# Moving a float64 weight conversion between two stages of a fused mLSTM, mixture-of-experts and gated MLP kernel, and letting one block's second products trail by two steps

## The chip, the core and the metric

The kernel runs on one core of a Trainium2 chip. The metric is the device time of one execution in microseconds (us), from the median of several runs. The engines are called by their short names: PE (TensorE, the matrix products), ACT (ScalarE), DVE (VectorE), POOL (GpSimd) and SP (SyncE, which here only issues transfers).

## What is computed

Three layers run one after the other on 3072 tokens of width 320. The change touches the second and the third; the first, a recurrent attention (mLSTM), is not touched.

```python
# second layer: eight experts, each token goes to one of them (x: 3072 x 320, F = 1024)
for e in range(E):
    mask = expert_idx == e
    h = np.maximum(x[mask] @ w1[e], 0.0)
    out[mask] = gate_w[mask, None] * (h @ w2[e])
...
# third layer: a gated MLP (w_in: 320 x 2048, w_out: 2048 x 320)
h = x @ w_in
g = h * (1.0 / (1.0 + np.exp(-1.702 * h)))
return (g @ w_out).astype(np.float32)
```

The third layer's weights `w_in` and `w_out` come as float64, because they are drawn in float32 and then multiplied by a float64 factor; the kernel has to turn their bits into float32 itself.

## The kernel before

All products are made in float32 accuracy from fp32r pieces: each operand is split into a rounded high part and a rest, and three products (high by high, high by low, low by high) are summed in PSUM. So every weight and every activation costs a copy on ACT (the high part) and a subtraction on DVE or POOL (the rest).

**Experts.** There are 64 steps `s`, eight experts `e` of eight steps `m`. The first four experts work on up to 512 tokens, the last four on up to 384 (`CAPS`). A step makes the first products of one slice of 128 hidden columns (`h_mm`, line 138, eight matmuls into the PSUM tile `hp`, of which there are two), then the relu and its split (`relu_split`: `hh` on ACT, line 1093, and `hl` on DVE, line 1094), then the second products of the slice of the step before (`tail`, `o_mm`, lines 1117 to 1119, into the PSUM tiles `acc`). After that the same step splits a weight slice for a later step (`split_w`: lines 105 and 118 on ACT, 110 on POOL, 111 and 121 on DVE), transposes the next expert's tokens in three of the eight steps (`prep_x`), and calls `convert`.

**Conversion.** `cvt_all` is a generator over the 16 column blocks of `w_in` and `w_out`. A block needs 10 pieces, five for its `w_in` part (128x384) and five for its `w_out` part (128x320); `convert(n)` runs the next n pieces. The first piece is `fr` and `es` on ACT (lines 1158 and 1161) with `ex` on DVE between them (line 1159; `es` reads `ex`); the other four are one DVE operation each (`mt` 1163, `fr` 1165, `es` 1167, `fr` 1169). When the fifth piece is done, the split of the finished weights is put on the list `late`, and the next `convert` runs it (the same lines 105 to 121, now into `win` and `wout`). The float64 words are loaded to the tile `c` by SP (line 1177), two such tiles in turn. In all 160 pieces: the experts run `convert(2 + m % 2)` for 512 tokens and `convert(1 + m % 2)` for 384, from step 2 on.

**Gated MLP.** Five blocks of 512 tokens and two of 256, each with 16 steps. A step of a block is `h_mm`, then `swish_split`: ACT makes the sigmoid `sg` (line 1104), DVE multiplies it with `hp` (line 1105, which frees `hp`), ACT rounds the product to `hh` (line 1106) and DVE subtracts for `hl` (line 1107). Then come the second products of an earlier step, taken from the list `left`. A step of a 512-token block costs PE eight first and twelve second matmuls. The first block, number `E`, runs what is left of the conversion beside its products, three pieces a step, and also prepares the second block: `scale_y` (line 1246, on POOL), and from the sixth step on `planes` (1268), `words` (1277) and `parts` (1285 and 1286).

Nothing here is ordered by a scheduler: under `tc.manual_schedule` each engine works through its instructions in the order in which the code is written, and waits on semaphores for what it reads or overwrites.

Of the kernel before, what the change touches and what calls it, by code (L numbers as in the profile page):

```python
# [20 lines left out]
CAP = 512  # L21
# [5 lines left out]
def kernel(ctx, tc, qT_in, kT_in, kvo_in, i_gate, f_gate, expert_emb, tau, w12, wio, out, dbg=None):  # L27
# [5 lines left out]
    E = expert_emb.shape[0]  # L33
# [18 lines left out]
    CAPS = [CAP] * (E // 2) + [CAP - P] * (E // 2)  # L52
# [33 lines left out]
    def load_w(g):  # L86

        p, m = divmod(2 * g, M1)
        r1, r2 = w_dma(ids[p], m // 2, rawp.tile([P, W2], F32, tag="r", name="r"))
        wraw[2 * g], wraw[2 * g + 1] = (r1[:, :, 0:P], r2[:, 0]), (r1[:, :, P:2 * P], r2[:, 1])  # L90
# [915 lines left out]
    with ExitStack() as mctx:  # L1006
# [16 lines left out]
        def load_x0(j):  # L1023

            if j:
                xr_t["first"] = xp.tile([P, NB, 3 * P], F32, tag="xr", name="xr", bufs=1)
                t = xr_t["first"][:, 0:NB // 2]
            else:
                t = mp2.tile([P, NB, DM], F32, tag="o", name="xr", bufs=1).rearrange("p i d -> p (i d)")
                t = t[:, 0:NB // 2 * 3 * P].rearrange("p (i d) -> p i d", d=3 * P)  # L1030
            xr_t["first", j] = t
            src = rows[ds(ids[0] * RS + j * EARLY, EARLY), :].rearrange("(i p) d -> p i d", p=P)
            nc.sync.dma_start(out=t[:, :, 0:DM], in_=src)
# [8 lines left out]
        ncol = lambda blk: GN if blk == "g" else COLS[blk]  # L1042
# [15 lines left out]
        def prep_x0(j, c):  # L1058

            if j and c == 0:  # L1060
                xh_t[0] = mp2.tile([P, 3, CAP], F32R, tag="xh", name="xh")
                xl_t[0] = mp2.tile([P, 3, CAP], F32R, tag="xl", name="xl")
            xh, xl, xr = xh_t[0], xl_t[0], xr_t["first", j]
            js = slice(2 * j * P, (2 * j + 2) * P)
            if c == 0:
                nc.scalar.copy(xr[:, :, DM:3 * P], xr[:, :, 2 * P:DM])
            pool, tag = (ps_h, "hp") if j and c == 2 else (ps_x, "xt")
            t = pool.tile([P, CAP], F32, tag=tag, name="xt")[:, 0:2 * P]
            for i in range(2):
                nc.tensor.transpose(t[:, i * P:(i + 1) * P], xr[:, i, c * P:(c + 1) * P], ident)  # L1070
            nc.scalar.copy(xh[:, c, js], t)
            nc.vector.tensor_tensor(out=xl[:, c, js], in0=t, in1=xh[:, c, js].bitcast(F32), op=ALU.subtract)

        def touch():

            xr, n = xr_t["first", 1], 3 * P - DM
            t = ps_x.tile([P, CAP], F32, tag="xt", name="xt")
            nc.tensor.matmul(t[:, 0:n], ident, ident[:, 0:n], start=True, stop=True)
# [300 lines left out]
        with tc.manual_schedule():  # L1379
            load_x0(1)  # L1380
            flag = nc.values_load(vals_i[0:1, 2 * E:2 * E + 1], min_val=0, max_val=1)
            with tc.If(flag > 0):
                general()
            touch()
            nc.vector.memset(exb, -896.0 * 2 ** 23)
            load_x0(0)
            for p in range(1, E):
                ids[p] = nc.values_load(vals_i[0:1, p:p + 1], engines=sp, min_val=0, max_val=E - 1)
                if p == 1:
                    load_w(WA // 2 + 1)  # L1390
                    for c in range(3):
                        prep_x0(1, c)
                    load_x(1)
                    load_w(WA // 2 + 2)
                    load_c(0)
                    load_c(1)
            offs = {p: nc.values_load(vals_i[0:1, E + p:E + p + 1], engines=sp, min_val=0, max_val=NT) for p in range(1, E)}

            steps = [(e, m, e * M1 + m) for e in range(E) for m in range(M1)]
            prev = None  # L1400
            conv = cvt_all()

            def convert(n):

                now, late[:] = late[:], []
                for f in now:
                    f()
                for _ in range(n):
                    next(conv, None)

            def tail(p):
                e, m, s = p
                o_mm(e, ("a", s), wslot.pop(s)[1], m == 0, m == M1 - 1)
                if m == M1 - 1:
                    put(e)

            for e, m, s in steps:
                h_mm(e, ("a", s), wslot[s][0], EARLY if s in he else 0)
                relu_split(("a", s))
                if s in he:  # L1420
                    hs_t["a", s] = halves(*he.pop(s)) + hs_t["a", s]
                if prev:
                    tail(prev)
                prev = (e, m, s)
                if 1 <= s < 4:
                    prep_x0(0, s - 1)
                if s == 1:
                    gts = gates_1()
                if s == 2:
                    gates_2(*gts)  # L1430
                if s == 3:
                    order_rows()
                if s == 4:
                    meta_tile()

                for w in [] if s == 0 else [s + WA - 1] if s < WA else [s + WA - 1, s + WA] if s == WA else [s + WA]:
                    if w < NS1:
                        split_w(w)
                        if w % 2 and w // 2 + 3 < NS1 // 2:
                            load_w(w // 2 + 3)  # L1440
                if e + 1 < E and 2 <= m - (e == 0) < 5:
                    prep_x(e + 1, m - 2 - (e == 0))
                if m == 5 + (e == 0) and e + 2 < E:
                    load_x(e + 2)
                if s % 2 == 0 and 0 <= s // 2 - 3 < NTILE:
                    meta_put(s // 2 - 3)
                if s == 7 + 2 * NTILE:
                    meta_get()
                if s == 9 + 2 * NTILE:
                    meta_split()  # L1450
                if e == E - 1:

                    if m == 1:
                        load_y(E)
                    if m == 3:
                        scale_y(E, nc.vector)
                    if 4 <= m < 7:
                        prep_x(E, m - 4)
                    if m == 7:
                        load_y(E + 1)  # L1460

                if s > 1:
                    convert((1 if CAPS[e] < CAP else 2) + m % 2)

            def tail2(p):
                blk, m = p
                o_mm(blk, ("b", blk, m), wout[:, m], m == 0, m == M2 - 1)
                if m == M2 - 1:
                    put_out(blk)

            left = [prev]
            for blk in range(E, len(COLS)):
                for m in range(M2):
                    h_mm(blk, ("b", blk, m), win[:, m])
                    swish_split(("b", blk, m))
                    left.append((blk, m))
                    while len(left) > (1 if ncol(blk) == CAP else 2):
                        p = left.pop(0)
                        (tail2 if len(p) == 2 else tail)(p)
                    if blk == E:  # L1480
                        convert(3)
                    nxt = blk + 1
                    if nxt < len(COLS):
                        t = m - (2 if blk == E else 0)
                        small = ncol(blk) < CAP
                        if t == 2:
                            scale_y(nxt, nc.vector if small else nc.gpsimd)
                        for j in range(ncol(nxt) // GH):
                            t0 = t - 3 * j
                            if 3 <= t0 < 5:  # L1490
                                planes(nxt, j, t0 - 3)
                            w0 = t0 - (8 if small else 6)
                            if 0 <= w0 < 2:
                                words(nxt, j, w0)
                            if 2 <= w0 < 5:
                                parts(nxt, j, w0 - 2)
                        if t == 8 and nxt + 1 < len(COLS):
                            load_y(nxt + 1)
            for p in left:
                tail2(p)  # L1500
            if dbg is not None:
                nc.sync.dma_start(out=dbg["slot"], in_=slot_i)
                nc.sync.dma_start(out=dbg["lg"], in_=logit_all.rearrange("p t e -> p (t e)"))
                nc.sync.dma_start(out=dbg["ss"], in_=ss_all)
# [62 lines left out]
```

## Time and profile before

| what | value |
|---|---|
| median of 3 runs | 808.52 us (808.39 to 808.96) |
| the profiled execution: its time, its span | 810.2 us, 808.5 us |
| PE busy | 751.4 us, 93% of the span |
| DVE, ACT, POOL busy | 564.4, 354.2, 249.8 us |
| granted TensorE clock, mean | 0.963 of full speed |

The span runs from the first to the last instruction that the profile shows; the execution's own time has 1.7 us more around it. The attention takes the first 205 us or so, the experts run from 210 to 437 us, the first gated block from 437 to 506 us, and the six other blocks fill the rest. Busy shares are averages over stages with different limits, so each stage is read by itself.

### The profile page before, as it was taken

Reading aid. Unit: us, or ns where it says so; the run is one execution under the profiler, and the core shown is the slowest. Engines: PE = TensorE matmul, PEld = TensorE weight load, DVE = VectorE, ACT = ScalarE, POOL = GpSimd, SP = SyncE. Lnnn points to the kernel's source line nnn. Section 1 sums busy time; section 2 is a strip of 40 time slices with the busy share of each in tenths; the row PEclk is TensorE's granted clock in tenths of the full one; section 3 lists DMA queues with packets and bytes.
Section 4 is the critical chain, followed back from the end, with each engine's and each line's share of the span. In section 5 each row is a group of like instructions: output and inputs, shape, how many; then the busy total and the mean of one; then the engine's idle time right before and its main releaser. Section 6 shows DMA issues by size and latency. Waiting matters only on the chain.

```text
span 808.5 us, 13134 instructions
## 1 busy us (share of the span) xinstructions
PE 751.4 (93%) x4708; PEld 692.6 (86%) x4708; DVE 564.4 (70%) x1146; ACT 354.2 (44%) x834; POOL 249.8 (31%) x362
## 2 busy tenths in 40 slices
PE   6899898898779999999999899999999999999995
PEld 6889798888768888889988687898989888899995
DVE  7877999997488888888976776554554454445542
ACT  4343334324356556565654444333334333334442
POOL 4653577775123343444520200300300300102011
PEclk9787999899899999999999999999999999999998
DMA  6976876652637637557843122120120110200100
GB/s 195 310 263 206 285 252 224 227 192 86 216 79 252 207 114 237 162 181 205 208 123 104 36 56 59 43 64 6 48 64 1 54 40 9 64 1 21 33 18 16
DMA packets 70303, 100.20 MB, mean 124 GB/s; under 512 B 31120, under 2 KB 56472, under 8 KB 70232
## 3 DMA queue, kind: packets, MB, share of 16 engines
q1 hardware_dynamic: 67160, 91.41, 37.2%
q0 software_dynamic: 3072, 7.89, 2.6%
q8 instruction: 38, 0.62, 0.3%
q14 instruction: 33, 0.27, 0.1%
HBM read 77.53 MB, written 17.82 MB: 118 GB/s over the span
## 4 chain that ended last, share of the span: by engine, by line
issue 37%; DVE 17%; PE 9%; ACT 5%; POOL 4%; DMA 1%; SPq 0%; POOLq 0%; DVEq 0%; ACTq 0%
PE hp L138 4%; DVE w L121 3%; POOL out_dram L1140 3%; DVE w L111 2%; PE acc L1119 2%; DVE hl L1094 2%; DVE es L1167 2%; PE acc L1118 1%; PE acc L1117 1%; DVE fr L1165 1%; ACT hh L1093 1%; DMA c<-in_wio_dram 1%; POOL xr L1246 1%; DVE ex L1159 1%; DVE xl L1056 1%
## 5 line engine op out<-in xcount | busy, mean ns | idle before, releaser
L1105 DVE TENSOR_TENSOR sg<-hp,sg 128x512 f32<-128x512 f32 (+1 forms) x112 | 68.8, 614 | 91.3 <-ACT sg L1104 84.9
L138 PE MATMUL hp<-xh,win 128*128 128x512 f32 (+1 forms) x560 | 131.5, 365 | 0.0
L1117 PE MATMUL acc<-wout,hhl 128*128 128x320 f32 x384 | 119.8, 312 | 4.4 <-ACT hhl L1106 4.3
L1119 PE MATMUL acc<-wout,hhl 128*128 128x320 f32 x384 | 120.4, 314 | 1.1 <-DVE hhl L1107 1.0
L1107 DVE TENSOR_TENSOR hhl<-sg,hhl 128x512 fp32r<-128x512 f32 (+1 forms) x112 | 71.3, 637 | 70.0 <-ACT hhl L1106 69.0
L1118 PE MATMUL acc<-wout,hhl 128*128 128x320 f32 x384 | 119.2, 310 | 0.0
L1104 ACT ACTIVATE sg<-hp 128x512 f32<-128x512 f32 (+1 forms) x112 | 60.0, 536 | 116.2 <-PE hp L138 116.2
L1140 POOL DMA_INDIRECT out_dram<-o,tokd x24 | 23.7, 987 | 273.5 <-ACT o L1127 269.7
L138 PEld LDWEIGHTS hp<-xh,win 128*128 128x128 f32 x560 | 94.3, 189 | 11.4
L1106 ACT CAST hhl<-sg 128x512 fp32r<-128x512 f32 (+1 forms) x112 | 62.6, 559 | 86.7 <-DVE sg L1105 83.2
L138 PE MATMUL hp<-xl,win 128*128 128x512 f32 (+1 forms) x336 | 85.6, 363 | 0.0
L110 POOL TENSOR_TENSOR w<-r,w 128x256 fp32r<-128x256 f32 x58 | 45.7, 788 | 124.5 <-ACT w L105 121.6
L1117 PEld LDWEIGHTS acc<-wout,hhl 128*128 128x128 f32 x384 | 72.7, 189 | 10.4 <-ACT hhl L1106 7.0
L138 PE MATMUL hp<-xh,w 128*128 128x384 f32 (+2 forms) x320 | 76.5, 370 | 0.0
L1119 PEld LDWEIGHTS acc<-wout,hhl 128*128 128x128 f32 x384 | 72.5, 189 | 3.6 <-DVE hhl L1107 3.5
L1118 PEld LDWEIGHTS acc<-wout,hhl 128*128 128x128 f32 x384 | 72.6, 189 | 3.5
L1119 PE MATMUL acc<-w,hl 128*128 128x320 f32 x212 | 68.2, 322 | 6.8 <-DVE hl L1094 6.6
L1117 PE MATMUL acc<-w,hh 128*128 128x320 f32 x212 | 66.5, 314 | 2.4 <-ACT hh L1093 2.4
L138 PEld LDWEIGHTS hp<-xl,win 128*128 128x128 f32 x336 | 58.8, 189 | 10.9 <-DVE xl L1286 0.2
L1118 PE MATMUL acc<-w,hh 128*128 128x320 f32 x212 | 65.7, 310 | 0.0
L360 DVE TENSOR_TENSOR_SCAN pm<-fb,ident_h 128x1024 f32<-128x1024 f32 x23 | 56.3, 2448 | 5.4 <-DMA fb<-dec 5.3
L400 PE MATMUL sp<-qT,kblk 120*128 120x128 f32 x384 | 56.4, 308 | 3.1 <-DVE wm L405 2.7
(315 smaller groups left out, 1522.8 us busy)
## 6 DMA issues: line engine op xcount, KB each, us to landing
r<-in_w_dram SPq DMA_DIRECT2D x32, 704.0 KB
fb<-dec SPq DMA_DIRECT2D x23, 512.0 KB
kvo<-in_kvo_dram SPq DMA_DIRECT2D x24, 480.0 KB
c<-in_wio_dram SPq DMA_DIRECT2D x16, 704.0 KB
rows<-zt SPq DMA_DIRECT2D x8, 640.0 KB
qT<-in_qT_dram SPq DMA_DIRECT2D x24, 180.0 KB
xr<-y SPq DMA_DIRECT2D x5, 640.0 KB
kblk<-in_kT_dram SPq DMA_DIRECT2D x48, 60.0 KB
```

What stands on the lines that cost most here:

```text
L110: eng.tensor_tensor(out=t[:, 3 * P:5 * P].rearrange("p (c f) -> p c f", c=2), in0=r1[:, 0:2], in1=hif[:, 0:2], op=ALU.subtract)
L138: nc.tensor.matmul(hp, a, b, start=(i == 0), stop=(i == len(seq) - 1))
L360: nc.vector.tensor_tensor_scan(out=pm[u].rearrange("p h t -> p (h t)"), data0=fb[u].rearrange("p h t -> p (h t)"), data1=ident_h.rearrange ...
L400: nc.tensor.matmul(sp[:, h - hs.start], kblk[u % NLD][0:KR, h // 3, h % 3, :], qT[u][0:KR, h // 3, :], start=True, stop=True)
L1104: nc.scalar.activation(out=sg, in_=hp, func=AF.Sigmoid, scale=1.702)
L1105: nc.vector.tensor_tensor(out=g, in0=hp, in1=sg, op=ALU.mult)
L1106: nc.scalar.copy(hh, g)
L1107: nc.vector.tensor_tensor(out=hl, in0=g, in1=hh.bitcast(F32), op=ALU.subtract)
L1117: nc.tensor.matmul(a, hh, w[:, 0:DM], start=first, stop=False)
L1118: nc.tensor.matmul(a, hh, w[:, DM:2 * DM], start=False, stop=False)
L1119: nc.tensor.matmul(a, hl, w[:, 0:DM], start=False, stop=last)
L1140: sc = nc.gpsimd.indirect_dma_start(out=out, out_offset=bass.IndirectOffsetOnAxis(ap=tokd[:, ti:ti + 1], axis=0), in_=o[:, i], in_offset=None)
```

## The change

Three numbers and one condition are edited. In the experts the conversion starts at step 4 instead of step 2, and a step runs 2 or 3 pieces by `m % 4 > 0` instead of `m % 2` (1 or 2 for the 384-token experts): three steps in four take the larger number, where it was one in two. In the first gated block a step runs two pieces instead of three. And in this block the list `left` keeps two steps instead of one, so that the second products come two steps behind the first ones; blocks 2 to 5 keep one, the two small ones keep two, as before.

```diff
@@ the loop over the experts' steps
-                if s > 1:
-                    convert((1 if CAPS[e] < CAP else 2) + m % 2)
+                if s > 3:
+                    convert((1 if CAPS[e] < CAP else 2) + (m % 4 > 0))
@@ the loop over the gated blocks
                     left.append((blk, m))
-                    while len(left) > (1 if ncol(blk) == CAP else 2):
+
+                    while len(left) > (1 if E < blk and ncol(blk) == CAP else 2):
                         p = left.pop(0)
                         (tail2 if len(p) == 2 else tail)(p)
                     if blk == E:
-                        convert(3)
+                        convert(2)
```

Counted out, the pieces stand so: before, 15 by the end of step 7, 123 by the end of the experts, and 37 in the first gated block; after, 11, 133 and 27.

What this does to the engines' own order is seen at three places. The first is PE at the passage from the experts to the first gated block (`win` is the gated layer's weight, `w` the experts'). Before:

```order
L1119 MATMUL acc<-w,hl 128x320
L138 MATMUL hp<-xh,win 128x512 x5
L138 MATMUL hp<-xl,win 128x512 x3
L1117 MATMUL acc<-w,hh 128x320
L1118 MATMUL acc<-w,hh 128x320
L1119 MATMUL acc<-w,hl 128x320
```

And now:

```order
L1119 MATMUL acc<-w,hl 128x320
L138 MATMUL hp<-xh,win 128x512 x5
L138 MATMUL hp<-xl,win 128x512 x3
L138 MATMUL hp<-xh,win 128x512 x5
L138 MATMUL hp<-xl,win 128x512 x3
L1117 MATMUL acc<-w,hh 128x320
L1118 MATMUL acc<-w,hh 128x320
L1119 MATMUL acc<-w,hl 128x320
```

The second step's first products now stand ahead of the last expert's second products, and from here to the block's end each step's second products have one more step of first products and one more of second products in front of them.

The second place is DVE in the experts' steps 3 and 4, a piece of the difference (a minus is before, a plus is now):

```order
 L121 TENSOR_TENSOR w<-r,w 128x320
 L1056 TENSOR_TENSOR xl<-xt,xh 128x512
-L1165 SCALAR_TENSOR_TENSOR fr<-mt,fr 128x384
-L1167 SCALAR_TENSOR_TENSOR es<-c,es 128x384
-L1169 TENSOR_TENSOR fr<-fr,es 128x384
 L1094 SCALAR_TENSOR_TENSOR hl<-hp,hh 128x256
 L1219 COPY metat<-tok_i 128x24
```

The three pieces of step 3 are gone from in front of step 4's `hl`; in the same way `ex` and `mt`, the pieces of step 2, are gone from in front of step 3's.

The third place is DVE at the start of the first gated block, from its first multiplication (line 1105) to its third. Before:

```order
L1105 TENSOR_TENSOR sg<-hp,sg 128x512
L1107 TENSOR_TENSOR hhl<-sg,hhl 128x512
L1125 COPY o<-acc 128x320
L1167 SCALAR_TENSOR_TENSOR es<-c,es 128x384
L1169 TENSOR_TENSOR fr<-fr,es 128x384
L1159 TENSOR_SCALAR ex<-c 128x320
L1105 TENSOR_TENSOR sg<-hp,sg 128x512
L1107 TENSOR_TENSOR hhl<-sg,hhl 128x512
L111 TENSOR_TENSOR win<-fr,win 64x128
L1163 TENSOR_SCALAR mt<-c 128x320
L1165 SCALAR_TENSOR_TENSOR fr<-mt,fr 128x320
L1167 SCALAR_TENSOR_TENSOR es<-c,es 128x320
```

And now:

```order
L1105 TENSOR_TENSOR sg<-hp,sg 128x512
L1107 TENSOR_TENSOR hhl<-sg,hhl 128x512
L1167 SCALAR_TENSOR_TENSOR es<-c,es 128x384
L1169 TENSOR_TENSOR fr<-fr,es 128x384
L1105 TENSOR_TENSOR sg<-hp,sg 128x512
L1107 TENSOR_TENSOR hhl<-sg,hhl 128x512
L1125 COPY o<-acc 128x320
L111 TENSOR_TENSOR win<-fr,win 64x128
L1159 TENSOR_SCALAR ex<-c 128x320
L1163 TENSOR_SCALAR mt<-c 128x320
```

One piece a step is gone between two multiplications, and the `ex` of the next column block follows the second step's `win` split instead of ending the first step.

## Rows read from the trace of the kernel before

**Rows 1.** Windows by stage: experts 1-3, experts 4-7, first gated block, second.

```profile
core 0: us, PE busy (x) PEld busy (x) DVE busy (x) ACT busy (x) POOL busy (x), PEclk, DMA share, GB/s
241.80:336.80 95.00, 94.14 (x515) 82.31 (x515) 82.38 (x161) 55.37 (x124) 37.26 (x54) 0.99 0.59 190
336.80:437.10 100.30, 95.55 (x587) 91.54 (x587) 83.28 (x166) 57.99 (x137) 37.33 (x54) 1.00 0.60 169
437.10:505.94 68.84, 63.34 (x320) 52.85 (x318) 49.85 (x93) 32.05 (x64) 6.06 (x5) 0.98 0.22 63
505.94:564.16 58.22, 58.22 (x323) 52.20 (x321) 29.94 (x49) 22.29 (x42) 6.94 (x9) 1.00 0.14 39
```

**Rows 2.** Waits in the first gated block: total us, times, longest.

```profile
PE acc L1117 <- ACT hhl L1106: 4.3, 5, 2.4
```

**Rows 3.** Timeline of the first gated block: start, length, engine, instruction, wait before.

```profile
459.12 2.80 POOL L1246 TENSOR_TENSOR xr<-xr,gated 128x1536 f32<-128x1536 f32 x1
459.32 2.78 DVE L1159 TENSOR_SCALAR ex<-c 128x320 int32<-128x320 int32 x1
464.61 0.42 PE L1117 MATMUL acc<-wout,hhl 128*128 128x320 f32 x1 [2.38 <-ACT hhl L1106]
475.71 0.69 DVE L1105 TENSOR_TENSOR sg<-hp,sg 128x512 f32<-128x512 f32 x1 [0.88 <-ACT sg L1104]
501.37 0.69 DVE L1105 TENSOR_TENSOR sg<-hp,sg 128x512 f32<-128x512 f32 x1 [0.39 <-ACT sg L1104]
505.01 0.69 DVE L1105 TENSOR_TENSOR sg<-hp,sg 128x512 f32<-128x512 f32 x1 [1.24 <-ACT sg L1104]
506.99 0.42 DVE L1286 TENSOR_TENSOR xl<-xt,xh 128x256 fp32r<-128x256 f32 x1
507.11 0.86 PE L138 MATMUL hp<-xl,win 128*128 128x512 f32 x3
```

**Rows 4.** DVE's groups in the first gated block: busy us, mean ns.

```profile
L1165 DVE SCALAR_TENSOR_TENSOR fr<-mt,fr 128x384 f32<-128x384 int32 (+1 forms) x8 | 4.2, 524 | 0.4
L1169 DVE TENSOR_TENSOR fr<-fr,es 128x384 f32<-128x384 f32 (+1 forms) x8 | 4.2, 522 | 0.2
L1167 DVE SCALAR_TENSOR_TENSOR es<-c,es 128x384 int32<-128x384 int32 (+1 forms) x8 | 4.1, 518 | 0.0
L111 DVE TENSOR_TENSOR win<-fr,win 64x128 fp32r<-64x128 f32 x4 | 2.8, 711 | 0.1
L1163 DVE TENSOR_SCALAR mt<-c 128x384 int32<-128x384 int32 (+1 forms) x8 | 2.7, 338 | 0.0
...
L121 DVE TENSOR_TENSOR wout<-fr,wout 128x320 fp32r<-128x320 f32 x4 | 1.9, 484 | 0.0
```

**Rows 5.** Windows around the longest wait of that block; columns as in rows 1.

```profile
464.00:467.00 3.00, 2.23 (x9) 1.96 (x10) 2.32 (x5) 1.50 (x3) 0.00 (x0) 0.76 0.11 17
467.00:470.00 3.00, 3.00 (x12) 2.62 (x11) 1.68 (x3) 1.59 (x4) 0.00 (x0) 0.67 0.87 279
```

**Rows 6.** Timeline of experts' steps 2 to 5: ACT, DVE and PE.

```profile
221.85 0.49 DVE L121 TENSOR_TENSOR w<-r,w 128x320 fp32r<-128x320 f32 x1
222.94 0.56 ACT L1158 ACTIVATE fr<-c 128x384 f32<-128x384 uint32 x1 [2.52 <-DMA c<-in_wio_dram]
224.30 0.42 DVE L1094 SCALAR_TENSOR_TENSOR hl<-hp,hh 128x256 fp32r<-128x256 f32 x1 [0.79 <-ACT hh L1093]
230.66 0.41 PE L1119 MATMUL acc<-w,hl 128*128 128x320 f32 x1 [2.45 <-DVE hl L1094]
```

**Rows 7.** Waits of PE from 204 to 250 us; then a window there.

```profile
PE acc L1119 <- DVE hl L1094: 4.3, 2, 2.5
...
240.00:245.00 5.00, 5.00 (x21) 4.43 (x21) 3.98 (x10) 1.86 (x4) 0.73 (x1) 0.66 0.66 96
```

**Rows 8.** Timeline of expert 4's third step: a first piece and the wait behind it.

```profile
344.85 0.56 ACT L1161 ACTIVATE es<-ex,exb 128x320 int32<-128x320 int32 x1 [2.69 <-DVE ex L1159]
345.84 0.41 PE L1117 MATMUL acc<-w,hh 128*128 128x320 f32 x1 [1.16 <-ACT hh L1093]
```

## The prediction

> **What bounds the kernel now.** I read the windows by stage first. In the second gated block PE is busy for all of its 58.22 us, 16 steps of 3.64 us; the first block does the same work (three second matmuls fewer) in 68.84 us, so about 11 us are lost there [rows 1]. In experts 1 to 7 PE is busy for 94.14 of 95.00 and 95.55 of 100.30 us: 5.6 us idle, with DVE busy for 165.7 of 195.3 us [rows 1]. The second block has no such idle time, and what comes after it is of the same kind, so whatever the first block saves, the end saves too.
>
> Then the waits. In the first gated block PE waits for `hhl`, the rounded activations that ACT writes for the second products, five times, 4.3 us in all [rows 2], the longest 2.38 us [rows 3]; in the timeline the reader sees why. POOL's `scale_y` runs for 2.80 us, and DVE's `ex`, begun 0.2 us later, takes 2.78 us; the sigmoid, the product and the rounding queue up behind it. The clock pays as well: in the 6 us after that wait it is granted at 0.76 and 0.67 [rows 5]. The rest of the 11 us is the same chain in small: sigmoid on ACT, product on DVE, rounding on ACT, rest on DVE, with three conversion pieces between two products.
>
> In expert 0, PE waits 4.3 us for `hl` [rows 7], 2.45 us of it once [rows 6], because ACT and DVE are late there.
>
> **Part 1: the conversion starts at step 4.** By the end of step 7 four pieces fewer have run. A column block of ten pieces costs DVE, by the means in [rows 4] and with `ex` priced like `mt`, 2 x (0.338 + 0.338 + 0.524 + 0.518 + 0.522) + 0.711 + 0.484 = 5.7 us, so 0.57 us a piece and 2.3 us for four. Besides, ACT's first `fr` waits 2.52 us for its data and holds up `hh`: DVE was through at 222.34 (221.85 + 0.49) but began `hl` at 224.30, 1.96 us later [rows 6]. Two steps later the data has long landed. Together 4.3 us; I take **4.0 us off**, since PE's own steps take over as the bound. Ends: 2.0 (only one of the two reaches PE) and 6.0 (the 4.3 us of PE's waits, and the 5 us at clock 0.66 that follow [rows 7], 1.7 us of them lost).
>
> **Part 2: denser conversion from step 8 on.** 122 pieces instead of 108, 14 x 0.57 = 8.0 us more on DVE, which is idle for 29.6 us in this stretch [rows 1]; so most fits, but not at the right moment. What hurts PE is a first piece: ACT's `es` waits for DVE's `ex`, `hh` stands behind `es`, and PE waited 1.16 us for that `hh` [rows 8]. First pieces in these steps go from 22 to 24; two more at 1.16 us are 2.3 us. I take **2.5 us on**, near that row. Ends: nothing (all in DVE's gaps) and 8.0 (all on the path).
>
> **Part 3: two pieces a step and a lag of two in the first gated block.** Both belong together. With the lag, PE reaches the second products of a step one whole step, 3.64 us, later, so a lateness of ACT and DVE up to that size is no wait any more; that alone covers the 2.38 us wait and the small ones. But a lag does not make the chain shorter, it only lends time. `hp` has two buffers, so the first products of step m+2 wait for DVE's product of step m, and at the end the second block's first products read the last `xl` that DVE makes behind the last step. So I take DVE's chain over the whole block. It ends at 507.41 (506.99 + 0.42), just in time for the low products at 507.11 [rows 3], 70.3 us after the block's start. Of these it waited 0.39 and 1.24 us for PE in the last two steps [rows 3]; 68.7 are its own. Ten pieces, one column block, leave it: 5.7 us, and up to two waits of 0.88 us behind an `es` [rows 3], so 5.7 to 7.5; I take 6.5, the middle. The chain then needs 62.2 us and ends at 499.3. The second block's first products began 1.5 us ahead of that end (505.94 against 507.41), so now they begin at 497.8, with one set of twelve second matmuls, half a step or 1.8 us, still to do: as if at 499.6, against 505.94. That is **6.3 us off**; PE alone would have been there 4.7 us sooner. Ends: 4.0 (the chain has waits of its own where two pieces fall badly) and 11 (all that is lost).
>
> The 2.4 us of the `scale_y` stall I leave in this chain. POOL does `scale_y` right behind the `win` split in its queue; that split now comes in the block's second step instead of its fifth, and in DVE's order an `ex` and a `mt` stand behind it there as before. The rule that speaks against the change is about this pair: the Trainium skill's "GPSIMD Engine Reference", section "Key points", says that the two engines share their SBUF interfaces and that DVE instructions in a two-port mode or with two SBUF inputs contend with POOL's. The trace agrees for `ex`: 2.78 us beside POOL [rows 3]. If only `ex` were held and another operation stood there, the sum would be 2.4 us lower, 798.3; by the page `fr`, `es` and the subtraction would be held as well, and the sum stays.
>
> **What costs nothing.** The last expert's second products and its `put` come one step later; their reader is a load nine steps on. The 16 loads of `c` on SP are as many as before; at 2.75 pieces a step a tile lasts 3.6 steps, about 14 us, so SP never brings them late, and if it did, ACT would wait as it does now, 2.5 us [rows 6]. POOL is idle for most of the first gated block, 6.06 of 68.84 us busy [rows 1], so its earlier split and `scale_y` delay nobody there but DVE. The lists and ring buffers gain no instruction.
>
> **Sum.** -4.0 + 2.5 - 6.3 = -7.8 us. The profiled execution took 810.2 us (span 808.5), which gives 802.4 for it; the median of the runs, 808.52, lies 1.7 below and gives **800.7 us**.
>
> **Rivals.**
> - *The lag hides everything.* DVE's chain is shorter than I add up, and the first gated block runs at PE's 3.64 us a step. For: the chain has fewer waits once PE is ahead. Against: even at 7.5 us for the ten pieces it ends 3.7 us late. 808.5 - 4.0 + 2.5 - 11 = 796.0. Chance 0.17.
> - *The wait moves to the second block's start and takes the clock down.* PE waits there some 4.7 us in one or several lumps; a wait of 2.38 us was followed by 6 us at 0.76 and 0.67 [rows 5], which lose 3 x 0.24 + 3 x 0.33 = 1.7 us. Time 802.4. Chance 0.17. The Trainium skill's "TensorE: Matmul & The Clock Gate", section "Part 1: The HAM clock gate", has the same rule, that an idle PE drops to half rate; on the 2.38 us wait the trace agrees.
> - *The experts pay in full.* All 8.0 us of the 14 pieces lie on the path: 808.5 - 4.0 + 8.0 - 6.3 = 806.2. Against: 29.6 us of gaps [rows 1]. Chance 0.15.
> - *Slower: first pieces at the end of a step.* Before, five pieces went into two steps of a 512-token expert, so a first piece always stood first in its step. Now it also stands last, behind two others; `ex` ends later, and with it `es` and `hh`. PE's idle time in experts 1 to 7 is 5.6 us for 22 first pieces, 0.25 each; the row at 1.16 us shows what a bad one costs [rows 8]. The gains of 10.3 us are gone when 24 of them cost (10.3 + 5.6) / 24 = 0.66 us on average; at 0.8 us it is 808.5 - 10.3 + 24 x 0.8 - 5.6 = 811.8. Chance 0.07.
>
> That the change does not do what it says is excluded by the order of the instructions, which shows the lag and the moved pieces.
>
> **How the numbers follow.** My forecast has what is left, 0.44. The predicted time is 800.7 us. The range goes from 795.5, just below the case in which all is hidden, to 806.5, just above the one in which the experts pay in full; outside it lie the slower rival and the joint extremes of the ends. A measurement tells 0.2% from no change, 1.6 us here. Faster by more than that: my case, the first two rivals, and most of the third, 0.85. Within: 0.08. Slower: 0.07.
>
> **What would show it.** In the new profile expert 0 ends about 4 us sooner, with no ACT wait for `c`; experts 1 to 7 take some 198 us instead of 195.3. In the first gated block PE's waits for `hhl` are nearly gone, replaced by waits of its first products for `hp` or, at the passage to the second block, for `xl`, together some 5 us; the block takes about 61 us. `ex` still shows one run of over 2 us beside POOL. I am wrong if the first block runs at PE's pace, if it keeps its 68.8 us, or if experts 1 to 7 grow by more than 8 us.

## The result and the profile after

The changed kernel took **812.39 us** (median of 12 runs, 808.11 to 817.77); the kernel before, run beside it on the same chip, took 808.45. The ratio is **1.006, interval 1.003 to 1.009**: slower, by 3.9 us by the medians and 4.9 by the ratio. The prediction was 800.7 us with a range to 806.5 and a chance of 0.07 for slower. It was wrong in sign and in range. The profiled execution took 812.8 us with a span of 811.1; that of before took 810.2 us with a span of 808.5.

The engines' busy times on its page:

```profile
PE 752.0 (93%) x4708; PEld 692.8 (85%) x4708; DVE 568.2 (70%) x1146; ACT 352.9 (44%) x834; POOL 248.2 (31%) x362
```

It hardly differs from the page of before (PE 751.4 us, 93%). The stages do. Windows of after: expert 0, experts 1 to 7, the first gated block with the second's first step, the next three steps (columns as in [rows 1]; PEld is PE's loading of the operand that stays in it during a product).

```profile
210.10:236.24 26.14, 25.23 (x169) 24.07 (x168) 20.23 (x50) 13.46 (x35) 7.66 (x10) 0.96 0.61 210
236.24:444.55 208.31, 195.16 (x1102) 174.53 (x1100) 175.39 (x345) 115.62 (x268) 74.27 (x109) 0.99 0.57 172
444.55:510.07 65.52, 62.49 (x339) 54.99 (x338) 47.61 (x87) 31.74 (x64) 5.58 (x5) 1.00 0.20 55
510.07:523.08 13.01, 11.17 (x62) 9.80 (x61) 6.79 (x6) 3.36 (x7) 6.54 (x9) 1.00 0.13 52
```

The same two middle stretches of before, and the three steps:

```profile
241.82:437.10 195.28, 189.67 (x1100) 173.83 (x1100) 165.64 (x326) 113.36 (x260) 74.59 (x108) 1.00 0.60 179
509.56:520.48 10.92, 10.92 (x63) 9.81 (x61) 5.72 (x8) 4.32 (x9) 6.94 (x9) 1.00 0.15 62
437.10:509.56 72.46, 66.96 (x340) 56.01 (x338) 51.57 (x96) 33.56 (x67) 6.06 (x5) 0.98 0.21 59
```

| stage | before | after | change | predicted |
|---|---|---|---|---|
| expert 0 | 31.78 | 26.14 | -5.6 | -4.0 |
| experts 1 to 7 | 195.28 | 208.31 | **+13.0** | +2.5 |
| first gated block, to the second's first step | 72.46 | 65.52 | -6.9 | -6.3 |
| the next three steps | 10.92 | 13.01 | +2.1 | 0 |

The changes sum to +2.6 us, which is the difference of the two spans. Two lines carry the miss; the other two came out 2.2 us better than forecast. Experts 1 to 7 are the first. PE is idle there for 208.31 - 195.16 = 13.2 us (before 5.6), and, the reverse of what I had assumed, **DVE is not fuller**: it is busy for 9.8 us longer and still stands idle for 32.9 us, where it was 29.6. The extra work went into no gap; the stage grew round it. The waits of this window (total us, times, longest) say at what:

```profile
ACT es L1161 <- DVE ex L1159: 65.2, 26, 5.8
DVE hl L1094 <- ACT hh L1093: 21.3, 25, 1.2
PEld acc L1119 <- DVE hl L1094: 17.1, 30, 1.2
PE acc L1119 <- DVE hl L1094: 8.9, 18, 0.9
PE xt L1054 <- issue: 2.1, 1, 2.1
```

And in the same stage of before:

```profile
ACT es L1161 <- DVE ex L1159: 46.7, 23, 4.6
DVE hl L1094 <- ACT hh L1093: 20.6, 23, 1.1
PEld acc L1119 <- DVE hl L1094: 6.6, 16, 0.8
PE acc L1119 <- DVE hl L1094: 2.3, 9, 0.6
```

From the bottom up: PE waits 8.9 us for DVE's `hl` instead of 2.3; two thirds of DVE's idle time, 21.3 of 32.9 us, lie right in front of `hl`, in waits for ACT's `hh`; and ACT, in front of that, sits for 65.2 us in `es`, waiting for DVE's `ex`. Here is one turn of it, from expert 1 (start, length, engine, instruction, wait before it):

```profile
248.71 0.55 DVE L1167 SCALAR_TENSOR_TENSOR es<-c,es 128x384 int32<-128x384 int32 x1
249.29 0.56 DVE L1169 TENSOR_TENSOR fr<-fr,es 128x384 f32<-128x384 f32 x1
249.77 0.32 DVE L1159 TENSOR_SCALAR ex<-c 128x320 int32<-128x320 int32 x1
250.13 0.56 ACT L1161 ACTIVATE es<-ex,exb 128x320 int32<-128x320 int32 x1 [4.01 <-DVE ex L1159]
250.59 0.58 ACT L1093 ACTIVATE hh<-hp 128x512 fp32r<-128x512 f32 x1
251.21 0.69 DVE L1094 SCALAR_TENSOR_TENSOR hl<-hp,hh 128x512 fp32r<-128x512 f32 x1 [1.12 <-ACT hh L1093]
...
253.70 1.48 DVE L111 TENSOR_TENSOR win<-fr,win 64x128 fp32r<-64x128 f32 x1
...
256.38 0.69 DVE L1094 SCALAR_TENSOR_TENSOR hl<-hp,hh 128x512 fp32r<-128x512 f32 x1
...
257.12 0.41 PE L1119 MATMUL acc<-w,hl 128*128 128x320 f32 x1 [0.71 <-DVE hl L1094]
```

The first piece stands last in its step, behind two others. ACT reaches `es` early and stands there 4.01 us; `hh` is behind it in ACT's queue; `hl` needs `hh`. So DVE, which has just made ACT wait, now waits 1.12 us for ACT, and everything behind `hl` in DVE's queue is later by that much. DVE loses more before the next `hl`: its subtraction at line 111 took 1.48 us, against 0.29 at 247.98, while POOL ran two of its own (line 110, 253.59 to 255.01). At the next step's `hl` the lateness from both reaches PE, 0.71 us.

The second line is in the second gated block. Timeline of after, POOL, DVE and PE:

```profile
514.20 3.61 DVE L1107 TENSOR_TENSOR hhl<-sg,hhl 128x512 fp32r<-128x512 f32 x1 [0.69 <-ACT hhl L1106]
514.50 2.76 POOL L1246 TENSOR_TENSOR xr<-xr,gated 128x1536 f32<-128x1536 f32 x1
517.87 0.42 PE L1119 MATMUL acc<-wout,hhl 128*128 128x320 f32 x1 [1.84 <-DVE hhl L1107]
```

POOL's next `scale_y` begins 0.30 us after DVE's `hhl`, which takes 3.61 us in place of its usual 0.69, and PE waits 1.84 us. Before, `scale_y` began when one of these subtractions was through. Only its last 0.9 us met the next one, which took 1.46 us, and PE did not wait (10.92 of 10.92 us busy above):

```profile
513.64 0.69 DVE L1107 TENSOR_TENSOR hhl<-sg,hhl 128x512 fp32r<-128x512 f32 x1 [0.69 <-ACT hhl L1106]
515.42 2.76 POOL L1246 TENSOR_TENSOR xr<-xr,gated 128x1536 f32<-128x1536 f32 x1
515.91 0.69 DVE L1105 TENSOR_TENSOR sg<-hp,sg 128x512 f32<-128x512 f32 x1 [1.57 <-issue]
517.28 1.46 DVE L1107 TENSOR_TENSOR hhl<-sg,hhl 128x512 fp32r<-128x512 f32 x1 [0.69 <-ACT hhl L1106]
```

The first gated block itself went much as the prediction drew it. The timeline rows that answer to [rows 3]:

```profile
453.57 2.80 POOL L1246 TENSOR_TENSOR xr<-xr,gated 128x1536 f32<-128x1536 f32 x1
453.77 2.78 DVE L1159 TENSOR_SCALAR ex<-c 128x320 int32<-128x320 int32 x1
...
505.46 0.50 PE L138 MATMUL hp<-xh,win 128*128 128x512 f32 x1 [1.53 <-ACT xh L1285]
505.75 0.42 DVE L1286 TENSOR_TENSOR xl<-xt,xh 128x256 fp32r<-128x256 f32 x1
```

All of PE's waits of 0.2 us or more in that block, which had 4.3 us for `hhl` before [rows 2]:

```profile
PE hp L138 <- ACT xh L1285: 1.5, 1, 1.5
PE hp L138 <- DVE sg L1105: 1.5, 2, 1.1
```

### The profile page after: what moved, and what is told of

It reads as the page before. It is cut to its first block, busy times and chain, and to the rows that moved or that the text cites. A ratio compares the mean times of both kernels' runs of the same rounds, so it can differ in the third digit from the quotient of the medians.

```text
span 811.1 us, 13161 instructions
## 1 busy us (share of the span) xinstructions
PE 752.0 (93%) x4708; PEld 692.8 (85%) x4708; DVE 568.2 (70%) x1146; ACT 352.9 (44%) x834; POOL 248.2 (31%) x362
## 4 chain that ended last, share of the span: by engine, by line
PE 26%; DVE 22%; issue 16%; ACT 6%; POOL 1%; DMA 1%; POOLq 0%; SPq 0%; DVEq 0%; ACTq 0%
PE hp L138 13%; PE acc L1119 4%; PE acc L1117 4%; PE acc L1118 4%; DVE w L121 4%; DVE w L111 3%; DVE es L1167 2%; DVE hl L1094 2%; DVE fr L1165 2%; DVE hhl L1107 2%; DVE xl L1056 1%; DVE sg L1105 1%; DVE fr L1169 1%; ACT hhl L1106 1%; ACT hh L1093 1%
## 5 line engine op out<-in xcount | busy, mean ns | idle before, releaser
L1107 DVE TENSOR_TENSOR hhl<-sg,hhl 128x512 fp32r<-128x512 f32 (+1 forms) x112 | 73.5, 656 | 70.0 <-ACT hhl L1106 70.0
L138 PEld LDWEIGHTS hp<-xh,w 128*128 128x128 f32 x320 | 55.2, 193 | 3.7
```

Source lines behind the costliest of these rows:

```text
L138: nc.tensor.matmul(hp, a, b, start=(i == 0), stop=(i == len(seq) - 1))
L1107: nc.vector.tensor_tensor(out=hl, in0=g, in1=hh.bitcast(F32), op=ALU.subtract)
```

## The experiments

**Theory A:** the denser pieces cost 13 us because of the loop DVE `ex`, ACT `es`, ACT `hh`, DVE `hl`; it is the order of the instructions, not the amount of work. **Rival B:** DVE has simply too much to do in the experts. **Rival C:** the loss comes from the later start, which shifts which piece falls into which step. Beside these: does the lag earn anything, and what does the collision in the second block cost?

All twelve runs in one table, times in us. The ratio is to the kernel before of the same comparison (its medians there were 808.31, 807.02 and 810.2, for e1 to e4, e5 to e8 and e9 to e12). The stages, each from one profiled execution, run from PE's first first-product of expert 0, of expert 1 and of the first gated block, the last one to the end of the span. The attention, which no edit touches, ended between 205.7 and 212.5 us in these executions, so spans alone are not compared.

| run | what it is | median | ratio, interval | expert 0 | experts 1-7 | gated to end |
|---|---|---|---|---|---|---|
| before | | 808.45 | 1 | 31.78 | 195.28 | 371.4 |
| after | | 812.39 | 1.006, 1.003 to 1.009 | 26.14 | 208.31 | 366.6 |
| e1 | later start alone | 804.61 | 0.996, 0.994 to 0.998 | 26.55 | 193.68 | 372.9 |
| e2 | density alone | 816.61 | 1.010, 1.006 to 1.013 | 31.15 | 206.29 | 366.1 |
| e3 | before, `es` put off | 789.49 | 0.977, 0.973 to 0.980 | 28.58 | 182.82 | 366.0 |
| e4 | after, `es` put off | 787.07 | 0.974, 0.972 to 0.976 | 26.36 | 186.39 | 363.1 |
| e5 | lag alone | 811.29 | 1.005, 1.002 to 1.008 | 30.65 | 195.11 | 373.6 |
| e6 | later start and lag | 808.61 | 1.002, 0.999 to 1.004 | 26.19 | 193.73 | 376.8 |
| e7 | e6, `es` put off | 790.79 | 0.981, 0.977 to 0.984 | 25.83 | 184.05 | 370.5 |
| e8 | e4, `scale_y` on DVE | 782.03 | 0.970, 0.966 to 0.973 | 26.03 | 186.68 | 360.6 |
| e9 | after, `scale_y` on DVE | 809.79 | 1.000, 0.998 to 1.003 | 26.34 | 208.67 | 363.7 |
| e10 | e8 without the lag | 785.23 | 0.969, 0.965 to 0.973 | 26.37 | 186.72 | 360.9 |
| e11 | e3, `scale_y` on DVE | 787.69 | 0.973, 0.970 to 0.977 | 28.79 | 182.78 | 365.3 |
| e12 | e8, the last expert's `y` a step later | 781.21 | 0.964, 0.961 to 0.967 | 25.56 | 184.35 | 361.6 |

**e1, the later start alone.**

```diff
-                if s > 1:
+                if s > 3:
```

> The kernel before with the conversion started at step 4 and nothing else; 42 pieces instead of 37 stay for the first gated block, three a step. If the two traces add up by stage (start: expert 0 gains 5.6 us; density: experts 1 to 7 lose 13 us), expert 0 (window from its first product to the second product of expert 1's first step) is 5 to 6 us shorter than before, experts 1 to 7 keep 195 us within 2, the first gated block grows by 5 pieces, 3 us: 806 us. Rival, that the late start itself shifts the pieces against the experts' steps and so makes experts 1 to 7 slow: they take 203 us or more, 814 us.

Expert 0 gains 5.2 us and experts 1 to 7 gain 1.6 with it, so the later start by itself is not what costs: C falls. Five pieces more now run in the first gated block, which gives 1.5 us back.

**e2, the density alone.**

```diff
-                    convert((1 if CAPS[e] < CAP else 2) + m % 2)
+                    convert((1 if CAPS[e] < CAP else 2) + (m % 4 > 0))
```

> The kernel before with m % 4 > 0 in place of m % 2 and nothing else: 17 pieces by step 7, 139 by the end of the experts, 21 for the first gated block. If the density is what costs, experts 1 to 7 take 205 to 210 us against 195, as in the changed kernel, expert 0 is 1 us longer, and the first gated block gains up to 10 us from 16 pieces fewer: 811 to 814 us. Rival, that the density costs little (my prediction, 2.5 us): experts 1 to 7 at 198 us, 801 us.

Experts 1 to 7 take 206.29 us, 11.0 more, and this kernel is the slowest of all. The loss belongs to the density. The time is above the 811 to 814 us that I expected, because the part behind the experts gained 5.3 us and not up to 10. The waits of `es` grow with it; the same rows of e1 (first two) and e2 (last two):

```profile
ACT es L1161 <- DVE ex L1159: 46.1, 23, 4.1
PE acc L1119 <- DVE hl L1094: 1.8, 6, 0.7
```

```profile
ACT es L1161 <- DVE ex L1159: 58.7, 25, 4.3
PE acc L1119 <- DVE hl L1094: 8.9, 13, 1.8
```

The two parts alone sum to -1.6 + 11.0 = +9.4 us in this stage; with both it was +13.0. Of the 3.6 us between, some 2.7 are the clock: before, the first 5 us of expert 1 were granted 0.81 (0.95 us lost); after, the 10 us from 431 us on were granted 0.82 and 0.83 (1.75 us lost), from the wait of 2.1 us in the `xt` row above on; in e1 and e2 the stage stands at 1.00. The last 0.9 us were not separated by any run.

**e3 and e4, `es` put off.** ACT's `es` goes onto the list `late` and runs at the start of the next `convert`, when `ex` has long been made; e3 is this edit in the kernel before, e4 in the changed one. No piece is removed.

```diff
-            nc.scalar.activation(out=es, in_=ex, func=AF.Relu, scale=float(2 ** 23), bias=exb)
+            late.append(lambda: nc.scalar.activation(out=es, in_=ex, func=AF.Relu, scale=float(2 ** 23), bias=exb))
```

> The kernel before, with the first piece's second ACT instruction (es, line 1161, which reads DVE's ex) put off to the start of the next convert, so that ACT does not wait for ex in front of the next step's hh or sigmoid. The same instructions, in another order on ACT. If ACT's wait for ex is what makes hl late and leaves DVE idle, DVE's idle time in front of hl (20.6 us in experts 1 to 7) falls to a few us, PE's waits there go from 5.4 to under 3 us, experts 1 to 7 take 188 to 192 us, the first gated block also gains 2 to 4 us: 800 us. If DVE's sheer load is the bound, nothing moves by more than 1.5 us: 808 us.

> The changed kernel with the same edit (es put off to the next convert). If the 13 us that experts 1 to 7 have lost come from ACT's wait for ex, which with three pieces in three steps of four stands behind more DVE work, they fall from 208 us to 198 us or less: 800 us or less. If they come from DVE's load (14 pieces more, DVE busy 9.8 us more), experts 1 to 7 stay above 204 us: 808 to 811 us.

This tells A from B. The window of experts 1 to 7 and its waits in e4:

```profile
238.85:425.24 186.39, 183.44 (x1101) 173.47 (x1100) 169.74 (x348) 118.07 (x268) 75.43 (x109) 1.00 0.67 192
```

```profile
ACT es L1161 <- DVE ex L1159: 4.7, 6, 1.8
DVE hl L1094 <- ACT hh L1093: 4.0, 8, 0.9
PE xt L1054 <- issue: 1.9, 1, 1.9
PE acc L1119 <- DVE hl L1094: 0.9, 1, 0.9
```

With the same 122 pieces the stage falls from 208.31 to 186.39 us. DVE has 169.74 us of work in it and finds room for it; ACT's wait goes from 65.2 to 4.7 us, DVE's wait for `hh` from 21.3 to 4.0, PE's for `hl` from 8.9 to 0.9. The step shown above reads like this in e4:

```profile
250.01 0.56 DVE L1169 TENSOR_TENSOR fr<-fr,es 128x384 f32<-128x384 f32 x1
250.49 0.32 DVE L1159 TENSOR_SCALAR ex<-c 128x320 int32<-128x320 int32 x1
250.72 0.69 DVE L1094 SCALAR_TENSOR_TENSOR hl<-hp,hh 128x512 fp32r<-128x512 f32 x1
...
252.49 0.56 ACT L1161 ACTIVATE es<-ex,exb 128x320 int32<-128x320 int32 x1
```

`hl` follows `ex` at once, since `hh` was made in time, and `es` comes 2 us later without a wait. B falls, A stands. A further rival, that DVE's operations were held beside POOL's (as line 111 was in the turn above), does not carry the 13 us: summed over the stage, DVE's operations took some 26 us more than the medians of their shapes in after, and 24 in before. e3 came out 10 us faster than expected. It shows that the loop was already in the kernel before: there the same edit takes 12.5 us off, down to a PE that is idle for 0.06 us:

```profile
240.21:423.03 182.82, 182.76 (x1102) 173.46 (x1100) 165.43 (x330) 113.83 (x258) 73.33 (x108) 1.00 0.69 192
```

So the price of the denser pieces is 13.0 us with `es` in the way and 186.39 - 182.82 = 3.6 us without. Of the 3.6, 1.9 are the one wait of the `xt` row above, in expert 7 (see e12).

**e5, the lag alone.**

```diff
-                    while len(left) > (1 if ncol(blk) == CAP else 2):
+                    while len(left) > (1 if E < blk and ncol(blk) == CAP else 2):
```

> The kernel before with the lag of two in the first gated block and nothing else; 37 pieces stay there, three a step. If DVE's chain over the block sets its end, the lag only moves PE's waits to the passage to the second block: the chain ends 0 to 2 us sooner after the block's start than before (70.3 us), and 807 to 810 us come out, the upper end if POOL's scale_y then meets the second block's hhl as in the changed kernel (3.6 us for one that takes 0.69). Rival, that the lag by itself hides the waits: the second block starts 5 us or more sooner and the time is 802 us or less.

The lag by itself costs 2.2 us after the experts, and the time is just above the expected range. PE's two largest waits in the first gated block and the first steps of the second:

```profile
PE hp L138 <- DVE sg L1105: 5.7, 5, 2.0
PE acc L1119 <- DVE hhl L1107: 1.8, 1, 1.8
```

The 4.3 us for `hhl` are gone and 5.7 us for `hp` stand in their place: the same lateness, met by the first products instead of the second ones, because `hp` has two buffers and its product on DVE is in the same chain. The 1.8 us are the collision with `scale_y`.

**e6 and e7, the later start with the lag, without and with `es` put off** (the edits of e1 and e5; of e1, e3 and e5).

> The late start and the lag, without the denser pieces: the experts' density and the three pieces a step of the first gated block as before (118 pieces by the end of the experts, 42 in the block). Start alone gave 804.6 us. If only shorter DVE work shortens the block, the lag adds nothing: 803 to 806 us, experts 1 to 7 at 194 us. If the lag by itself is worth something, 800 us or less.

> The late start and the lag with es put off to the next convert, density and three pieces a step as before. Against the changed kernel with es put off (787.1 us): if the denser pieces still cost in the experts, its experts 1 to 7 stand at 183 us as in the kernel before with es put off, 3.6 us less than 186.4, and the first gated block is 3 to 4 us longer for 15 pieces more: 786 to 788 us. If density costs nothing once es is out of the way, experts 1 to 7 are equal and this kernel is slower: 790 us.

e6 takes 3.9 us more than e1 behind the experts and loses all that e1 had gained; 803 to 806 us was expected, 808.61 came. In e7 the stage falls from 193.73 to 184.05 us, 9.7 us for the edit that took 12.5 off in e3. e4 beside e7 shows what moving the pieces is worth once `es` is out of the way: 2.3 us lost in experts 1 to 7 (186.39 against 184.05), 7.4 us gained behind them (363.1 against 370.5), and ratios of 0.974 and 0.981 whose intervals do not touch. Then it pays.

**e8 to e11, `scale_y` of the gated blocks on DVE.** POOL then has only the splits of `win` (line 110) left beside DVE there, in the first block. e8 and e9 have it in e4 and in the changed kernel, e11 in e3; e10 is e8 with the lag taken out again.

```diff
-                            scale_y(nxt, nc.vector if small else nc.gpsimd)
+                            scale_y(nxt, nc.vector)
```

> The changed kernel with es put off and with scale_y of the gated blocks on DVE instead of POOL (1.76 us there by the row of expert 7, against 2.8 us on POOL). If POOL's scale_y holds DVE's ex (2.78 us instead of 0.35) in the first block and hhl (3.6 instead of 0.69) in the second, both long runs are gone, the second block's 5.7 us step is back at 3.64, and the time falls by about 2 us, 785 us. Rival, that those long runs have another cause or that 1.76 us more on DVE cost as much: 787 us or more.

> The changed kernel with scale_y of the gated blocks on DVE, es where it was. The second block's subtraction, held for 3.6 us in all four kernels with the lag and scale_y on POOL, and in none without the lag, should take 0.69 us, its step 3.64 instead of 5.7 us: 2 us there; the first block's ex 0.35 instead of 2.78 us, partly paid back by 1.76 us on DVE: another 0 to 2 us. In all 808 to 810 us, against 812.4, with experts 1 to 7 still at 208 us. Rival, that the lag's loss (4 us in the run of the lag alone) is not the collision: 812 us.

> The changed kernel with es put off and scale_y on DVE, but without the lag (one step behind, as before). If the lag is worth something once the collision is gone and DVE's chain is shorter than PE's work, this kernel is 2 to 6 us slower than the same with the lag (782.0 us): 784 to 788 us, with waits of PE for hhl in the first gated block. If the chain alone sets the block's end, it is equal: 782 us.

> The kernel before with es put off and scale_y on DVE, nothing of the change. It tells what the whole change is worth once ACT no longer waits and POOL no longer collides: if 5.5 us from expert 0, 3 to 5 us from the first gated block and minus 3.6 us in experts 1 to 7 hold, it takes 787 to 789 us, 5 to 7 us more than the changed kernel with both edits (782.0). Rival, that the change gives nothing even then: 782 us.

In e8 the part behind the experts takes 2.5 us less than in e4. In e9 no subtraction is held any more, and that part falls from 366.6 to 363.7 us, 2.1 us of it in the second block's first steps. The ratio goes from 1.006 to 1.000, with intervals just apart, so the two collisions with `scale_y`, the old one and the new, cost the changed kernel some 3 us by the stages and up to 5 by the ratio. Only the new one, 2.1 us, is the change's own: the kernel before pays for the old one too. e8 and e10 differ by 0.0004 in the ratio, with intervals 0.007 wide: with the collision out of the way, lag or no lag is not told apart. e11 beside e3 gives a ratio of 0.973 against 0.977, with intervals that overlap: the old collision alone is worth too little to be measured. e11 beside e8 tells what the whole change is worth with both obstacles gone: by the stages it gains 2.8 us in expert 0 and 4.7 behind the experts and loses 3.9 between, and the ratios, 0.973 and 0.970, have intervals that overlap. So the forecast gain of 7.8 us was not there even then.

**e12, the last expert's `y` one step later.** In e4 and e8 PE waited once in expert 7, 1.9 and 2.1 us, in its transposes, whose tokens come from a load of `y` and DVE's scaling. e12 is e8 with both one step later.

```diff
-                    if m == 3:
+                    if m == 4:
                         scale_y(E, nc.vector)
-                    if 4 <= m < 7:
-                        prep_x(E, m - 4)
+                    if 5 <= m < 8:
+                        prep_x(E, m - 5)
```

> The changed kernel with es put off, scale_y on DVE, and the last expert's scale_y and the three transposes of the first gated block's tokens one step later (steps 4 and 5 to 7 instead of 3 and 4 to 6). DVE waits 3 us there for the load of y and PE 2.1 us behind it; one step is 2.7 us. If this wait is the latency of the store and load alone, it is gone and expert 7 takes 23 us instead of 25.7: 780 us. Rival, that the transposes then end too near the first gated block and the wait only moves to its first products: 782 us or more.

Expert 7 falls from 25.74 (e8) to 23.29 us and the stage to 184.35, but 1.0 us comes back behind it. At 0.964 (0.961 to 0.967) it is the fastest version found, 3.6% below the kernel before; its interval just overlaps that of e8, so the last step is likely, not certain.

## Why the prediction was wrong, point by point

**Part 1, right and undersized.** Expert 0 gained 5.6 us (4.0 predicted, end 6.0). PE's waits for `hl` there fell from 4.3 [rows 7] to 0.9 us. The clock, which I had only in the upper end, rose from 0.93 to 0.96 over the stage, some 1.1 us more. e1 confirms the part alone, 5.2 us.

**Part 2 is the step that failed:** "so most fits", with 2.5 us taken and 8.0 as the upper end. It measured +13.0 us. The 14 pieces were costed as work (8.0 us) to be laid into DVE's 29.6 us of idle time. But 20.6 of these 29.6 us were waits for `hh`, and `hh` waited for DVE: this was not room, it was the other half of the loop. A piece put ahead of `ex` lengthens ACT's wait and thereby DVE's own next wait. The upper end was wrong for the same reason, since it priced work alone. I had the rows: the 2.69 us `es` wait and the 1.16 us it cost PE [rows 8]. I multiplied them by **two new** first pieces and did not ask where in its step each one stands. Counted out, 14 of the 24 now stand behind one or two other pieces, where three of 22 did. In the traces ACT waited 3.2 us on average for each of these 14 and 1.7 for each of the ten that stand first (before: 2.3 for the three, 2.0 for the 19). What the denser pieces cost once `es` is out of the way is 1.5 us (e12 against e3) to 3.6 (e4 against e3). That this lies around my 2.5 is luck: the 2.5 was the price of two waits, not of the work.

**The slower rival had the mechanism:** first pieces behind two others, `ex` later, `es` and `hh` with it. Its price was close too. I asked for 0.66 us a first piece on average; PE's idle time became 13.2 us, 13.2 / 24 = 0.55, and PE's own matmuls took 5.5 us longer (1102 records against 1100). Only 0.8 us of that are the clock, by the losses given under e2. The rest is most likely waiting that the busy time hides: the loads of `hl` into PE waited 17.1 us for DVE instead of 6.6, an increase larger than that of the products behind them, and in e4 the same matmuls take 183.44 us in place of 195.16. That the rival's 811.8 us came so near the measured 812.4 is in part luck, since it had neither this nor the collision in the second block. A chance of 0.07 was far too low for a mechanism that the order of the instructions showed plainly and whose row was at hand.

**Part 3, the size right, the credit wrong.** The chain was forecast to take 62.2 us from the block's start; it took 505.75 + 0.42 - 444.55 = 61.6. The block gained 6.9 us against 6.3, `ex` took its 2.78 us at the forecast place, and PE's waits moved to `hp` and to the passage into the second block, as said, though to 3.0 us in all and not some 5, and there to ACT's `xh` and not DVE's `xl`. But I wrote that lag and fewer pieces "belong together" and that the lag "alone covers the 2.38 us wait". e5 shows the lag alone gaining nothing, and e8 against e10 shows no gain beside the fewer pieces that can be measured. The gain goes with the pieces: e2, without the lag, has 16 fewer there and is 5.3 us faster over the same stretch. Two pieces a step were not run alone, so that part is not separated. And the ten pieces that left the block are among the 14 that cost the experts 13 us.

**What costs nothing:** here I missed the second `scale_y`. I followed the first one to its new place and never asked where the next block's would fall; a term put at nothing measured 2.1 us. All five kernels with the lag and `scale_y` on POOL show the subtraction held for 3.6 us or more there (five, where the expectation of e9 counts four), none of the four without the lag does.

**The other rivals.** The clock did not fall at the second block (1.00 in both windows); the lag did not hide everything. The experts paid more than in full, and with it came one of the three signs that I had set for being wrong: experts 1 to 7 grew by more than 8 us.

## What to carry to other kernels

Before idle time is counted as room, look at what ends it: if it ends with another engine that was itself waiting for this one, it is part of a loop, and work added there can cost more than it lasts: here an estimated 8 us of work cost 13. In an in-order queue, an instruction that needs another engine's latest result should not stand ahead of one that the critical chain needs; putting it off by one step was worth 2.3% in the kernel before (e3), where the change as a whole lost 0.6%. The lag in the second products gained nothing here, because the first products were held by the same chain, and it shifted later work into a new collision, which has to be followed too.

## What the hardware showed that I had not expected

DVE operations beside POOL's `scale_y` (2.76 to 2.80 us) were held until it was through or a little longer: `ex` 2.78 us instead of 0.32, and in e1, e6 and e7 the conversion's `fr` (line 1165) 2.94 us, against about 0.5 elsewhere. New was that one that begins *before* POOL's is held as well: `hhl`, begun 0.30 us earlier, took 3.61 us and ended 0.55 us after it. In the kernel before, the one that met only POOL's last 0.9 us ended 0.56 us after it (517.28 + 1.46 against 515.42 + 2.76). In both, what counted was when POOL's operation ended, not which of the two had begun first. The multiplication with `hp`, whose one input is in PSUM, took its normal 0.69 us in the middle of POOL's (at 515.91 in the timeline of before above). The Trainium skill's "GPSIMD Engine Reference", section "Key points", names a contention with DVE instructions that use a two-port mode or have two SBUF inputs. The trace agrees for `hhl` and `fr`, and the multiplication fits as one that has only a single SBUF input. `ex` has a single one too and was held; whether it ran in a two-port mode no row here shows.
